# First modulation rows in three column blocks, the fourth row tile moved into the value stage, the last output tile in two pieces

## Chip, cores and metric

One core of one Trainium2 chip runs the whole program. The metric is the device time of one execution in microseconds (us); the profile's span, from the first to the last instruction, is about 2 us shorter.

Ratios in this document are the mean time of one kernel's fast runs over the mean time of the other's fast runs of the same rounds, so not quite the ratio of the medians that are quoted.

## The reference

A diffusion-style block: a modulated LayerNorm, linear attention with 32 heads, and a modulated SwiGLU. There are 2048 rows of width 1024; weights are bf16. Only the first half matters here.

```python
mod = (silu(c) @ w_mod).reshape(1, 6, 1, -1)      # w_mod: 1024 x 6144
sa, ca, ga, sb, cb, gb = mod[:, 0], ...           # shift, scale, gate, twice
h = layernorm(x) * (1 + ca) + sa
q, k, v = split(h @ wqkv)                         # each 2048 x 1024
# phi(q) and phi(k), kv = phi(k)^T v, o = phi(q) kv / (phi(q) z), then @ wo
x = x + ga * attention
h = layernorm(x) * (1 + cb) + sb
x = x + gb * ((silu(h @ w_gate) * (h @ w_up)) @ w_down)
```

No key, value or query can be made before `ca` and `sa` are known, and these need 4.2 MB of `w_mod`. That is what the first 25 us of the kernel are about.

## The kernel before

The rows are worked in four chunks (`sc`) of 512, each of four row tiles (`t`) of 128. All input transfers are issued on one queue, in the order of this code. `wme` holds columns of `w_mod`: first the scale (q = 1), then the shift (q = 0), in two blocks of 512 columns.

```python
for st in range(STC - 1):          # row tiles 0, 1, 2 of x
    load_x(st, nc.sync)
for b in range(2):
    for q in (1, 0):
        t = big("wme", [DC, NB])
        nc.sync.dma_start(out=t[:], in_=wm_v[:, :, q * D + b * NB:q * D + (b + 1) * NB])
    ...                            # rows 4b .. 4b+3 of the key weights, wk
    if b == 0:
        load_x(STC - 1, nc.sync)   # row tile 3
wv = load_w(wqkv_v, 2 * D, "wv")   # then x of the next chunk, then wq
```

The first stage. `in_order` pins the order of the instructions on DVE, ACT and POOL to the order of the code. `keep_warm` issues matmuls whose result nobody reads ("fillers"). `mod_block` turns one block of `w_mod` into columns of `ca1T` or `saT`, by matmuls with one moving column each. `k_mms` accumulates the six key groups of row tiles 0 to 2, one 128-wide slice `cc` of the width at a time. `modulate` applies scale and shift to one such slice on DVE.

```python
keep_warm(accs[5], 26)
with in_order(nc.vector, nc.scalar, nc.gpsimd):
    ...                            # LayerNorm and transposes of row tiles 0-2, 3 x keep_warm(4)
    for b in range(2):
        mod_block(b, 1); keep_warm(idle, 2)
        mod_block(b, 0); keep_warm(idle, 3)
        for cc in range(4 * b, 4 * b + 4):
            modulate(hTs[0], cc, ca1T, saT, 0, 3 * P)
        if b == 0:
            xn3 = ln1_norm(*ln1_stats(0, 3))
            k_mms(0, gs, accs, 0, 4)
            pe_transpose_tile(hTs[0], xn3, 3)
        else:
            k_mms(0, gs, accs, 4, 8)
    ...                            # modulate row tile 3, its two key groups
    k_evac(0, gs, accs)            # phi: exp on ACT, then two DVE instructions
    k_evac(0, gs2, accs2)
...
v_phase(0)                         # eight value groups of chunk 0
with tc.issue_after(last_on[nc.vector.engine]):
    ln1(1)                         # LayerNorm of chunk 1: behind the last key evacuation on DVE
q_phase(0, 0, 6)
modulate_all(hTs[1], ca1T, saT)
q_phase(0, 6, 8)                   # then the keys of chunk 1
```

The last stage, `down`, writes each output tile in two pieces of 512 columns: a series of 28 matmuls, a multiply and an add on DVE, a store.

Of the kernel before, what the change touches and what calls it, by code (L numbers as in the profile page):

```python
# [21 lines left out]
def kernel(  # L22
# [74 lines left out]
    def mm(out, lhsT, rhs, start, stop):  # L97
        return tc.keep_in_program_order(nc.tensor.matmul(out, lhsT=lhsT, rhs=rhs, start=start, stop=stop))  # L98
# [4 lines left out]
    def big(name, shape):  # L103
        return k8.tile([P] + shape, BF16, name=name, tag="k8")

    def acc_a():
        return pa.tile([P, NB], F32, name="acc", tag="pa")

    def acc_b(name, shape=(NB,), dt=F32):
        return pb.tile([P] + list(shape), dt, name=name, tag="pb")  # L110
# [8 lines left out]
    def load_x(st, eng):  # L119
        x_sb = k2.tile([P, D], BF16, name="x_sb")  # L120
        eng.dma_start(out=x_sb[:], in_=x2[st * P:(st + 1) * P, :])
        x_tiles[st] = x_sb

    for st in range(STC - 1):
        load_x(st, nc.sync)

    wme = []
    wk = [big("wk", [4, D]), big("wk", [4, D])]
    for b in range(2):
        ts = []  # L130
        for q in (1, 0):
            t = big("wme", [DC, NB])
            nc.sync.dma_start(out=t[:], in_=wm_v[:, :, q * D + b * NB:q * D + (b + 1) * NB])
            ts.append(t)
        wme.append(ts)
        for i in range(2):
            nc.sync.dma_start(out=wk[b][:, 2 * i:2 * i + 2, :], in_=wqkv_v[:, 4 * b + 2 * i:4 * b + 2 * i + 2, D:2 * D])
        if b == 0:
            load_x(STC - 1, nc.sync)

    def load_w(view, lo, name):
        ts = []
        for h in range(2):
            t = big(name, [4, D])
            nc.sync.dma_start(out=t[:], in_=view[:, 4 * h:4 * h + 4, lo:lo + D])
            ts.append(t)
        return ts
# [84 lines left out]
    def ln1_norm(sc, t, x_sb, mv, rstd):  # L232
        xn = k2.tile([P, D], BF16, name="xn", bufs=4)
        if sc == 0:
            normalise(xn[:], x_sb[:], mv[:, 0, 0:1], rstd[:, 0:1])
            return xn
        normalise_act(xn[:], x_sb[:], mv, rstd)
        nc.sync.dma_start_transpose(hTs[sc][:, :, t * P:(t + 1) * P], xn[:])
# [4 lines left out]
            ln1_norm(*ln1_stats(sc, t))  # L243

    def mod_block(b, q):
        k = 1 - q
        for i in range(4):
            col = q * DC + 4 * b + i
            for j in range(DC):
                mm(mod_ps[:, col:col + 1], lhsT=wme[b][k][:, j, i * P:(i + 1) * P],  # L250
                   rhs=scT[:, j:j + 1], start=(j == 0), stop=(j == DC - 1))
        cs = slice(4 * b, 4 * b + 4)
        src = mod_ps[:, q * DC + 4 * b:q * DC + 4 * b + 4]
        if q == 1:
            nc.vector.tensor_scalar_add(out=ca1T[:, cs], in0=src, scalar1=1.0)
        else:
            nc.vector.tensor_copy(out=saT[:, cs], in_=src)

    last_phi = [None]

# [17 lines left out]
    def k_evac(sc, gs, accs):  # L278
        for (t, nb), acc in zip(gs, accs):
            phi_to(pks[sc][:, t, nb * NB:(nb + 1) * NB], acc[:])  # L280

    def k_phase(sc, lo, hi):
        if lo == 0:
            pks[sc] = big("pk", [STC, D])
        for g in k_groups[lo:hi]:
            accs = [acc_a()]
            k_mms(sc, [g], accs)
            k_evac(sc, [g], accs)

    def v_phase(sc):  # L290
        v = big("v", [STC, HG, VW])
        vs[sc] = v
        nc.gpsimd.memset(v[:, :, :, P:VW], 1.0)
        for t in range(STC):
            for nb in range(NNB):
                acc = acc_a()
                for cc in range(DC):
                    mm(acc[:], lhsT=hTs[sc][:, cc, t * P:(t + 1) * P],
                                     rhs=wv[cc // 4][:, cc % 4, nb * NB:(nb + 1) * NB],
                                     start=(cc == 0), stop=(cc == DC - 1))  # L300
                nc.scalar.copy(out=v[:, t, nb * 4:(nb + 1) * 4, 0:P], in_=acc[:].rearrange("p (g e) -> p g e", e=P))  # L301

    def q_phase(sc, lo=0, hi=DC):
        if lo == 0:
# [94 lines left out]
    def keep_warm(acc, n):  # L399
        for _ in range(n):  # L400
            mm(acc[:], lhsT=sel[:, 0, :], rhs=sel[:], start=True, stop=True)

    gs = k_groups[0:6]
    accs = [acc_a() if i < 4 else acc_b("acc") for i in range(6)]
    keep_warm(accs[5], 26)
    hTs[0] = big("hT", [DC, SCW])
    pks[0] = big("pk", [STC, D])
    with in_order(nc.vector, nc.scalar, nc.gpsimd):
        st0 = ln1_stats(0, 0)
        st1 = ln1_stats(0, 1)  # L410
        xn0 = ln1_norm(*st0)
        st2 = ln1_stats(0, 2)
        xn1 = ln1_norm(*st1)
        pe_transpose_tile(hTs[0], xn0, 0)
        xn2 = ln1_norm(*st2)
        keep_warm(accs[5], 4)
        pe_transpose_tile(hTs[0], xn1, 1)
        keep_warm(accs[5], 4)
        pe_transpose_tile(hTs[0], xn2, 2)
        keep_warm(accs[5], 4)  # L420
        mod_ps = acc_b("mod_ps")
        for b in range(2):
            idle = accs[5] if b == 0 else accs2[0]
            mod_block(b, 1)
            keep_warm(idle, 2)
            mod_block(b, 0)
            keep_warm(idle, 3)
            for cc in range(4 * b, 4 * b + 4):
                modulate(hTs[0], cc, ca1T, saT, 0, 3 * P)
            if b == 0:  # L430
                xn3 = ln1_norm(*ln1_stats(0, 3))
                k_mms(0, gs, accs, 0, 4)
                pe_transpose_tile(hTs[0], xn3, 3)
                accs2 = [acc_b("acc")]
            else:
                k_mms(0, gs, accs, 4, 8)
        for cc in range(DC):
            modulate(hTs[0], cc, ca1T, saT, 3 * P, SCW)
        gs2 = k_groups[6:8]
        accs2.append(acc_b("acc"))  # L440
        k_mms(0, gs2, accs2)
        k_evac(0, gs, accs)
        k_evac(0, gs2, accs2)
    nc.vector.tensor_copy(out=sc32[:], in_=scT[:].unsqueeze(2).to_broadcast([P, DC, 32]))
    build_masks()

    for sc in range(NSC):
        if sc > 0:
            k_phase(sc, 0, 2)
            kv_phase(sc - 1)  # L450
            if sc >= 2:
                row = mod_rows(blks)
            k_phase(sc, 2, 4)
            if sc == 2:
                mod_bc(row)
            if sc == 3:
                mod_cols(row)
            k_phase(sc, 4, 8)
            if sc == 1:
                blks = mod_load([2 * D, 2 * D + NB, 5 * D, 5 * D + NB])  # L460
            if sc == 2:
                blks = mod_load([3 * D, 3 * D + NB, 4 * D, 4 * D + NB])
        v_phase(sc)
        if sc + 1 < NSC:
            with tc.issue_after(last_on[nc.vector.engine] if sc == 0 else last_phi[-5].ins):
                ln1(sc + 1)
        if sc == 0:
            q_phase(0, 0, 6)
        if sc + 1 < NSC:
            with tc.issue_after(last_phi[0].ins):  # L470
                modulate_all(hTs[sc + 1], ca1T, saT)
        if sc == 0:
            q_phase(0, 6, 8)
        if sc + 2 < NSC:
            for st in range((sc + 2) * STC, (sc + 3) * STC):
                load_x(st, nc.sync)
        if sc == 2:
            wo = load_w(wo_v, 0, "wo")
            for cc in range(DC):
                w = wo[cc // 4][:, cc % 4, :]  # L480
                nc.vector.tensor_tensor(out=w, in0=w, in1=ga_bc, op=ALU.mult)
# [89 lines left out]
    def down(sc, side):  # L571
        for t in range(STC):
            st = sc * STC + t
            for nb in range(NNB):
                ns = slice(nb * NB, (nb + 1) * NB)
                x1r = x1p.tile([P, NB], F32, name="x1r", bufs=2)
                nc.sync.dma_start(out=x1r[:], in_=x1_dram[st * P:(st + 1) * P, ns])
                y_ps = acc_a()
                for f in range(FC):
                    mm(y_ps[:], lhsT=guT[sc][f // GPT][:, f % GPT, t * P:(t + 1) * P],  # L580
                                     rhs=wd[f // WDF][:, f % WDF, ns], start=(f == 0), stop=(f == FC - 1))
                yt = ep.tile([P, NB], F32, name="e")
                nc.vector.tensor_tensor(out=yt[:], in0=y_ps[:], in1=gb_bc[:, ns], op=ALU.mult)  # L583
                ob = yp.tile([P, NB], BF16, name="ob")
                nc.vector.tensor_tensor(out=ob[:], in0=yt[:], in1=x1r[:], op=ALU.add)  # L585
                nc.sync.dma_start(out=out2[st * P:(st + 1) * P, ns], in_=ob[:])
                if side:
                    with tc.issue_after(last_mm[sc].ins):
                        side.pop(0)()
# [62 lines left out]
```

## Time and profile before

| | |
|---|---|
| time, median of 3 | 848.03 us (847.9 to 848.06) |
| span of the profile | 846.2 us |
| TensorE (PE) busy | 838.6 us |
| first key matmul | 16.30 us |
| value stage | 33.92 to 47.73 us |
| keys of chunk 1 | from 61.55 us |

The first part of the page of the kernel before gives, for each engine, busy time, share of the span and number of instructions.

```profile
PE 838.6 (99%) x4284; PEld 385.7 (46%) x4284; DVE 307.2 (36%) x602; ACT 173.8 (21%) x267; POOL 55.7 (7%) x160
```

TensorE is busy nearly always: the waits view of the whole span has only 0.6 us of PE waits after the first 25 us, so the rest of the program, 780 of 846 us, has hardly a wait to lose. But busy is not useful: fillers and waits that were filled count as busy. The timeline of PE shows that. Its columns are start and duration in us, engine, line, operation, output and inputs, tile sizes, number of instructions, and in brackets the idle time before and what ended it.

```profile
16.30 5.35 PE L98 MATMUL acc<-wk,hT 128*128 128x512 bf16 x24
21.49 0.61 PE L101 MATMUL tp<-ident,xn 128*128 128x128 bf16 x8
21.93 0.94 PE L98 MATMUL mod_ps<-scT,wme 128*128 128x1 bf16 x32
23.23 0.59 PE L98 MATMUL acc<-sel 128*128 128x512 bf16 x2 [0.35 <-DVE hT L221]
23.66 0.94 PE L98 MATMUL mod_ps<-scT,wme 128*128 128x1 bf16 x32
24.46 0.81 PE L98 MATMUL acc<-sel 128*128 128x512 bf16 x3
25.27 8.81 PE L98 MATMUL acc<-wk,hT 128*128 128x512 bf16 x40
33.92 13.98 PE L98 MATMUL acc<-wv,hT 128*128 128x512 bf16 x64
47.73 13.98 PE L98 MATMUL acc<-hT,wq 128*128 128x512 bf16 x64
61.55 3.62 PE L98 MATMUL acc<-wk,hT 128*128 128x512 bf16 x16
```

`acc<-sel` are fillers. Between 21.5 and 25.3 us TensorE makes no key: it turns row tile 3, makes the second modulation block, and fills.

How fast the transfers come sets this stage. The trace has the completion of every transfer, one semaphore step for each of 16 DMA engines; this list, worked out from those steps, has the last of the sixteen:

```
kernel before: landed at (us)
x tiles 0-2   4.04  4.81  5.51
wme 512 cols  9.38 (scale 0)   13.65 (shift 0)   20.01 (scale 1)   22.96 (shift 1)
wk, in halves of 4 rows: 15.01 16.40 | 24.31 25.67       x tile 3  17.09
wv            28.38  31.04
```

The LayerNorm of chunk 1 ends in transposes that the DMA queue does. This is the timeline of SP, which issues the transfers; the duration is that of the issue.

```profile
46.80 2.26 SPq L238 DMA_TRANSPOSE hT<-xn  x1
49.15 0.53 SPq L121 DMA_DIRECT2D x_sb<-in_A_x_dram  x1
49.77 1.24 SPq L238 DMA_TRANSPOSE hT<-xn  x1
```

These are the third transpose, a load of x that stands between, and the fourth and last; the first had been issued at 42.78. The last one landed at 53.35 us, 15.4 us after the first statistics of that LayerNorm (37.90 us), and long before the keys of chunk 1 at 61.55.

The end of the timeline, the last multiply and add on DVE:

```profile
841.77 0.69 DVE L583 TENSOR_TENSOR e<-acc,gb_bc 128x512 f32<-128x512 f32 x1 [4.63 <-PE acc L98]
842.49 0.69 DVE L585 TENSOR_TENSOR ob<-e,x1r 128x512 bf16<-128x512 f32 x1
```

### The profile page before, as it was taken

How to read it: one execution, taken by the hardware profiler on the slowest of the kernel's cores; microseconds unless marked ns; L12 is line 12 of the kernel's file. 1: busy time of each engine (PE TensorE's matmuls, PEld its weight loads, DVE VectorE, ACT ScalarE, POOL GpSimd, SP SyncE). 2: the span in 40 equal slices, each digit the busy share in tenths (PEclk: the TensorE clock that was granted, in tenths of full speed). 3: DMA queues.
4: the chain of work that ended last, by engine and by line, in shares of the span. 5: the costliest groups of instructions: out<-in, count | busy, mean ns of one | idle time of the engine just before them, and what ended most of it. 6: DMA issues, size and time to landing. Idle time of an engine off the chain costs nothing.

```text
span 846.2 us, 10498 instructions
## 1 busy us (share of the span) xinstructions
PE 838.6 (99%) x4284; PEld 385.7 (46%) x4284; DVE 307.2 (36%) x602; ACT 173.8 (21%) x267; POOL 55.7 (7%) x160
## 2 busy tenths in 40 slices
PE   8999999999999999999999999999999999999997
PEld 4445445544444444444444444444444444444443
DVE  5756464467423325431111344211114431111121
ACT  1455453354311110101111010011110101111000
POOL 2101010012011001100000010000001100000000
PEclk9999999999999999999999999999999999999999
DMA  9893870029976765528434073581604639710011
GB/s 309 301 257 98 243 187 1 1 52 215 348 210 207 214 186 174 181 69 266 146 104 149 19 236 95 159 283 54 199 1 126 185 69 318 240 59 0 19 57 50
DMA packets 125840, 128.74 MB, mean 152 GB/s; under 512 B 33376, under 2 KB 107360, under 8 KB 125280
## 3 DMA queue, kind: packets, MB, share of 16 engines
q1 hardware_dynamic: 122208, 115.36, 46.0%
q0 software_dynamic: 3584, 12.72, 5.0%
q8 instruction: 33, 0.54, 0.3%
q14 instruction: 15, 0.12, 0.0%
HBM read 108.01 MB, written 12.71 MB: 143 GB/s over the span
## 4 chain that ended last, share of the span: by engine, by line
PE 98%; DVE 1%; POOL 0%; DMA 0%; issue 0%; ACT 0%; SPq 0%; DVEq 0%; POOLq 0%
PE acc L98 88%; PE a_ps L98 7%; PE kvp L98 1%; PE modr L98 0%; PE wf L98 0%; DMA x_sb<-in_A_x_dram 0%; DVE stats L199 0%; PE mod_ps L98 0%; PE den L98 0%; POOL zmask L186 0%; PE tp L101 0%; POOL rstd L193 0%; PE bcr L98 0%; DVE e L583 0%; DVE ob L585 0%
## 5 line engine op out<-in xcount | busy, mean ns | idle before, releaser
L98 PE MATMUL acc<-h2T,wgu 128*128 128x512 bf16 x1792 | 387.9, 379 | 0.0
L98 PEld LDWEIGHTS <-wgu 128*128 128x128 bf16 x1792 | 175.1, 98 | 211.0
L98 PE MATMUL acc<-wd,gu 128*128 128x512 bf16 x896 | 196.0, 379 | 0.0
L566 DVE TENSOR_TENSOR gu<-acc,e 128x512 bf16<-128x512 f32 x112 | 77.4, 691 | 300.4 <-PE acc L98 300.4
L565 ACT ACTIVATE e<-acc 128x512 f32<-128x512 f32 x112 | 66.9, 597 | 375.2 <-PE acc L98 375.2
L98 PEld LDWEIGHTS <-gu 128*128 128x128 bf16 x896 | 87.6, 98 | 105.8
L98 PEld LDWEIGHTS <-hT 128*128 128x128 bf16 x512 | 49.6, 98 | 60.8 <-DVE hT L212 1.0
L583 DVE TENSOR_TENSOR e<-acc,gb_bc 128x512 f32<-128x512 f32 x32 | 22.1, 691 | 130.5 <-PE acc L98 130.5
L98 PE MATMUL a_ps<-wo,pq 128*128 128x512 bf16 x256 | 57.9, 379 | 0.6 <-DVE pq L395 0.6
L98 PE MATMUL acc<-hT,wq 128*128 128x512 bf16 x256 | 57.1, 379 | 0.0
L98 PE MATMUL acc<-wk,hT 128*128 128x512 bf16 x256 | 56.9, 379 | 0.0
L98 PE MATMUL acc<-wv,hT 128*128 128x512 bf16 x256 | 55.9, 379 | 0.0
L263 ACT ACTIVATE eb<-acc 128x512 bf16<-128x512 f32 x64 | 37.9, 596 | 62.8 <-PE acc L98 60.5
L209 ACT ACTIVATE xn<-x,nmr,rstd 128x1024 bf16<-128x1024 f32 x16 | 19.8, 1240 | 127.6 <-POOL nmr L207 127.6
L264 DVE TENSOR_SCALAR eb<-eb 128x512 bf16<-128x512 bf16 x64 | 18.4, 291 | 60.6 <-ACT eb L263 60.6
L98 PEld LDWEIGHTS <-pq 128*128 128x128 bf16 x256 | 24.7, 98 | 31.8 <-DVE pq L395 2.6
L98 PEld LDWEIGHTS <-wq 128*128 128x128 bf16 x256 | 24.9, 98 | 29.8
L534 POOL DMA_DIRECT2D x_scratch<-x x16 | 9.6, 600 | 369.6 <-DVE x L527 369.6
L527 DVE TENSOR_TENSOR x<-a_ps,x_sb 128x512 f32<-128x512 f32 x32 | 22.1, 691 | 8.0 <-PE a_ps L98 7.9
L193 POOL TENSOR_TENSOR rstd<-veps,neg_half 128x1 f32<-128x1 f32 x32 | 18.2, 569 | 81.3 <-DVE veps L191 70.4
L301 ACT CAST v<-acc 128x512 bf16<-128x512 f32 x32 | 18.3, 582 | 22.1 <-PE acc L98 22.1
L528 DVE BATCH_NORM_STATS2 stats<-x 128x6 f32<-128x512 f32 x32 | 22.2, 695 | 1.1
(72 smaller groups left out, 280.7 us busy)
## 6 DMA issues: line engine op xcount, KB each, us to landing
wgu<-in_B_w_gate_dram SPq DMA_DIRECT2D x28, 1024.0 KB, 7.4
wgu<-in_B_w_up_dram SPq DMA_DIRECT2D x28, 1024.0 KB, 8.7
x_sb<-in_A_x_dram SPq DMA_DIRECT2D x32, 256.0 KB, 5.9
wml<-in_w_mod_dram SPq DMA_DIRECT2D x8, 1024.0 KB, 8.6
x_scratch<-x POOLq DMA_DIRECT2D x16, 512.0 KB, 3.1
x1r<-x_scratch SPq DMA_DIRECT2D x32, 256.0 KB, 3.0
wd<-in_B_w_down_dram SPq DMA_DIRECT2D x7, 1024.0 KB, 7.7
wme<-in_w_mod_dram SPq DMA_DIRECT2D x4, 1024.0 KB, 11.2
```

The source lines that it names most:

```text
L98: return tc.keep_in_program_order(nc.tensor.matmul(out, lhsT=lhsT, rhs=rhs, start=start, stop=stop))
L193: nc.gpsimd.tensor_tensor(out=rstd[:, 0:n], in0=veps[:, 0:n], in1=neg_half[:].to_broadcast([P, n]), op=ALU.pow)
L209: nc.scalar.activation(out=dst, in_=src, func=ACT.Identity, bias=nmr[:], scale=rstd[:, 0:1])
L263: nc.scalar.activation(out=e[:], in_=acc, func=ACT.Exp)
L264: nc.vector.tensor_scalar(out=e[:], in0=e[:], scalar1=1.0, scalar2=PHI_EPS, op0=ALU.min, op1=ALU.add)
L301: nc.scalar.copy(out=v[:, t, nb * 4:(nb + 1) * 4, 0:P], in_=acc[:].rearrange("p (g e) -> p g e", e=P))
L527: nc.vector.tensor_tensor(out=x1[:, ns], in0=a_ps[:], in1=x_t[:, ns], op=ALU.add)
L528: nc.vector.bn_stats(out=stats[:, nb, :], in_=x1[:, ns])
L534: nc.gpsimd.dma_start(out=x1_dram[st * P:(st + 1) * P, :], in_=x1[:])
L565: nc.scalar.activation(out=sg[:], in_=ps[0][:], func=ACT.Silu)
L566: gm = nc.vector.tensor_tensor(out=guT[sc][f // GPT][:, f % GPT, :], in0=ps[1][:], in1=sg[:], op=ALU.mult)
L583: nc.vector.tensor_tensor(out=yt[:], in0=y_ps[:], in1=gb_bc[:, ns], op=ALU.mult)
```

## The change

The intent is to start keys sooner and to leave fewer of them behind the last modulation piece. The scale and shift columns come in blocks of three, three and two slices of 128 columns, each followed by the key-weight rows that need them, and the modulation of the next block stands before the last slice of the present one. Row tile 3 no longer takes part in the first key groups: its x is loaded between the two halves of `wv`, four value groups of tiles 0 and 1 are made first, and its transpose and two key groups come in the middle of the value stage. Twenty of the 48 fillers go. The masks, which POOL had made during the first LayerNorm, come later. The last tile's second piece is made in two halves.

```diff
+    MBLK = [(0, 3), (3, 6), (6, 8)]
-    for b in range(2):
+    for lo, hi in MBLK:
         for q in (1, 0):
-            nc.sync.dma_start(out=t[:], in_=wm_v[:, :, q * D + b * NB:q * D + (b + 1) * NB])
+            nc.sync.dma_start(out=ts[q][:], in_=wm_v[:, :, q * D + lo * P:q * D + hi * P])
+        ...                                   # the key-weight rows lo .. hi
-        if b == 0:
-            load_x(STC - 1, nc.sync)
 [in load_w]
+            if name == "wv" and h == 1:
+                load_x(STC - 1, nc.sync)
 [first stage]
-    keep_warm(accs[5], 26)
+    keep_warm(accs[5], 22)
-        keep_warm(accs[5], 4)                 # three times
+        keep_warm(accs[5], 3)                 # twice
+        mod_block(0, 1)
         pe_transpose_tile(hTs[0], xn2, 2)
+        mod_block(0, 0)
+        for b, (lo, hi) in enumerate(MBLK):
+            for cc in range(lo, hi):
+                modulate(hTs[0], cc, ca1T, saT, 0, 3 * P)
+            k_mms(0, gs, accs, lo, hi - 1)
+            if b + 1 < len(MBLK):
+                mod_block(b + 1, 1)
+                mod_block(b + 1, 0)
+            k_mms(0, gs, accs, hi - 1, hi)
+        st3 = ln1_stats(0, 3)
+        k_evac(0, gs[0:2], accs[0:2])
+        xn3 = ln1_norm(*st3)
+        k_evac(0, gs[2:], accs[2:])
+    ...                                       # value groups (0,0) (0,1) (1,0) (1,1), in two halves
+    pe_transpose_tile(hTs[0], xn3, 3)
+    ...                                       # modulate tile 3; values (2,*); keys of tile 3; values (3,*)
+    with tc.issue_after(last_on[nc.gpsimd.engine]):
         build_masks()
 [down]
+            pieces = [(0, NB), (NB, NB)]
+            if st == ST - 1:
+                pieces = [(0, NB), (NB, NB // 2), (NB + NB // 2, NB // 2)]
```

More of the change, by code (lines that the diff above doesn't have):

```diff
@@ L125 @@
         load_x(st, nc.sync)
+    MBLK = [(0, 3), (3, 6), (6, 8)]
     wme = []
     wk = [big("wk", [4, D]), big("wk", [4, D])]
-    for b in range(2):
-        ts = []
+    for lo, hi in MBLK:
+        ts = {}
         for q in (1, 0):
-            t = big("wme", [DC, NB])
-            nc.sync.dma_start(out=t[:], in_=wm_v[:, :, q * D + b * NB:q * D + (b + 1) * NB])
-            ts.append(t)
+            ts[q] = big("wme", [DC, (hi - lo) * P])
+            nc.sync.dma_start(out=ts[q][:], in_=wm_v[:, :, q * D + lo * P:q * D + hi * P])
         wme.append(ts)
-        for i in range(2):
-            nc.sync.dma_start(out=wk[b][:, 2 * i:2 * i + 2, :], in_=wqkv_v[:, 4 * b + 2 * i:4 * b + 2 * i + 2, D:2 * D])
-        if b == 0:
-            load_x(STC - 1, nc.sync)
+        for h in range(2):
+            r0, r1 = max(lo, 4 * h), min(hi, 4 * h + 4)
+            if r0 < r1:
+                nc.sync.dma_start(out=wk[h][:, r0 - 4 * h:r1 - 4 * h, :], in_=wqkv_v[:, r0:r1, D:2 * D])
     def load_w(view, lo, name):
@@ L245, in mod_block @@
     def mod_block(b, q):
-        k = 1 - q
-        for i in range(4):
-            col = q * DC + 4 * b + i
+        lo, hi = MBLK[b]
+        mod_ps = acc_b("mod_ps")
+        for i in range(hi - lo):
             for j in range(DC):
-                mm(mod_ps[:, col:col + 1], lhsT=wme[b][k][:, j, i * P:(i + 1) * P],
+                mm(mod_ps[:, i:i + 1], lhsT=wme[b][q][:, j, i * P:(i + 1) * P],
                    rhs=scT[:, j:j + 1], start=(j == 0), stop=(j == DC - 1))
-        cs = slice(4 * b, 4 * b + 4)
-        src = mod_ps[:, q * DC + 4 * b:q * DC + 4 * b + 4]
         if q == 1:
-            nc.vector.tensor_scalar_add(out=ca1T[:, cs], in0=src, scalar1=1.0)
+            nc.vector.tensor_scalar_add(out=ca1T[:, lo:hi], in0=mod_ps[:, 0:hi - lo], scalar1=1.0)
         else:
-            nc.vector.tensor_copy(out=saT[:, cs], in_=src)
+            nc.vector.tensor_copy(out=saT[:, lo:hi], in_=mod_ps[:, 0:hi - lo])
     last_phi = [None]
@@ L288, in k_phase, with new_v, v_mms, v_evac @@
             k_evac(sc, [g], accs)
+    def new_v():
+        v = big("v", [STC, HG, VW])
+        nc.gpsimd.memset(v[:, :, :, P:VW], 1.0)
+        return v
+    def v_mms(sc, t, nb, acc, lo=0, hi=DC):
+        for cc in range(lo, hi):
+            mm(acc[:], lhsT=hTs[sc][:, cc, t * P:(t + 1) * P], rhs=wv[cc // 4][:, cc % 4, nb * NB:(nb + 1) * NB],
+               start=(cc == 0), stop=(cc == DC - 1))
+    def v_evac(sc, t, nb, acc):
+        nc.scalar.copy(out=vs[sc][:, t, nb * 4:(nb + 1) * 4, 0:P], in_=acc[:].rearrange("p (g e) -> p g e", e=P))
+    def v_group(sc, t, nb, acc):
+        v_mms(sc, t, nb, acc)
+        v_evac(sc, t, nb, acc)
     def v_phase(sc):
-        v = big("v", [STC, HG, VW])
-        vs[sc] = v
-        nc.gpsimd.memset(v[:, :, :, P:VW], 1.0)
+        vs[sc] = new_v()
         for t in range(STC):
             for nb in range(NNB):
-                acc = acc_a()
-                for cc in range(DC):
-                    mm(acc[:], lhsT=hTs[sc][:, cc, t * P:(t + 1) * P],
-                                     rhs=wv[cc // 4][:, cc % 4, nb * NB:(nb + 1) * NB],
-                                     start=(cc == 0), stop=(cc == DC - 1))
-                nc.scalar.copy(out=v[:, t, nb * 4:(nb + 1) * 4, 0:P], in_=acc[:].rearrange("p (g e) -> p g e", e=P))
+                v_group(sc, t, nb, acc_a())
     def q_phase(sc, lo=0, hi=DC):
@@ L415 @@
         xn2 = ln1_norm(*st2)
-        keep_warm(accs[5], 4)
+        keep_warm(accs[5], 3)
         pe_transpose_tile(hTs[0], xn1, 1)
-        keep_warm(accs[5], 4)
+        keep_warm(accs[5], 3)
+        mod_block(0, 1)
         pe_transpose_tile(hTs[0], xn2, 2)
-        keep_warm(accs[5], 4)
-        mod_ps = acc_b("mod_ps")
-        for b in range(2):
-            idle = accs[5] if b == 0 else accs2[0]
-            mod_block(b, 1)
-            keep_warm(idle, 2)
-            mod_block(b, 0)
-            keep_warm(idle, 3)
-            for cc in range(4 * b, 4 * b + 4):
-                modulate(hTs[0], cc, ca1T, saT, 0, 3 * P)
-            if b == 0:
-                xn3 = ln1_norm(*ln1_stats(0, 3))
-                k_mms(0, gs, accs, 0, 4)
-                pe_transpose_tile(hTs[0], xn3, 3)
-                accs2 = [acc_b("acc")]
-            else:
-                k_mms(0, gs, accs, 4, 8)
+        mod_block(0, 0)
@@ new lines @@
+        for b, (lo, hi) in enumerate(MBLK):
+            for cc in range(lo, hi):
+                modulate(hTs[0], cc, ca1T, saT, 0, 3 * P)
+            k_mms(0, gs, accs, lo, hi - 1)
[7 more added lines that the diff above has]
+        k_evac(0, gs[2:], accs[2:])
+    vs[0] = new_v()
+    vg = [(0, 0, acc_b("acc")), (0, 1, acc_b("acc")), (1, 0, acc_a()), (1, 1, acc_a())]
@@ L437 @@
+    for half in range(2):
+        for t, nb, acc in vg:
+            v_mms(0, t, nb, acc, 4 * half, 4 * half + 4)
+    for t, nb, acc in vg:
+        v_evac(0, t, nb, acc)
+    pe_transpose_tile(hTs[0], xn3, 3)
+    with in_order(nc.vector):
         for cc in range(DC):
             modulate(hTs[0], cc, ca1T, saT, 3 * P, SCW)
-        gs2 = k_groups[6:8]
-        accs2.append(acc_b("acc"))
-        k_mms(0, gs2, accs2)
-        k_evac(0, gs, accs)
-        k_evac(0, gs2, accs2)
-    nc.vector.tensor_copy(out=sc32[:], in_=scT[:].unsqueeze(2).to_broadcast([P, DC, 32]))
@@ L445 @@
-    build_masks()
+    v_group(0, 2, 0, acc_a())
+    v_group(0, 2, 1, acc_a())
+    with in_order(nc.vector):
+        k_phase(0, 6, 8)
+    v_group(0, 3, 0, acc_a())
+    v_group(0, 3, 1, acc_a())
+    with tc.issue_after(last_on[nc.vector.engine]):
+        nc.vector.tensor_copy(out=sc32[:], in_=scT[:].unsqueeze(2).to_broadcast([P, DC, 32]))
+    with tc.issue_after(last_on[nc.gpsimd.engine]):
+        build_masks()
     for sc in range(NSC):
@@ L462 @@
                 blks = mod_load([3 * D, 3 * D + NB, 4 * D, 4 * D + NB])
-        v_phase(sc)
+            v_phase(sc)
         if sc + 1 < NSC:
@@ L573, in down @@
             st = sc * STC + t
-            for nb in range(NNB):
-                ns = slice(nb * NB, (nb + 1) * NB)
+            pieces = [(0, NB), (NB, NB)]
+            if st == ST - 1:
+                pieces = [(0, NB), (NB, NB // 2), (NB + NB // 2, NB // 2)]
+            for lo, width in pieces:
+                ns = slice(lo, lo + width)
                 x1r = x1p.tile([P, NB], F32, name="x1r", bufs=2)
-                nc.sync.dma_start(out=x1r[:], in_=x1_dram[st * P:(st + 1) * P, ns])
+                nc.sync.dma_start(out=x1r[:, 0:width], in_=x1_dram[st * P:(st + 1) * P, ns])
                 y_ps = acc_a()
                 for f in range(FC):
-                    mm(y_ps[:], lhsT=guT[sc][f // GPT][:, f % GPT, t * P:(t + 1) * P],
-                                     rhs=wd[f // WDF][:, f % WDF, ns], start=(f == 0), stop=(f == FC - 1))
+                    mm(y_ps[:, 0:width], lhsT=guT[sc][f // GPT][:, f % GPT, t * P:(t + 1) * P],
+                       rhs=wd[f // WDF][:, f % WDF, ns], start=(f == 0), stop=(f == FC - 1))
                 yt = ep.tile([P, NB], F32, name="e")
-                nc.vector.tensor_tensor(out=yt[:], in0=y_ps[:], in1=gb_bc[:, ns], op=ALU.mult)
+                nc.vector.tensor_tensor(out=yt[:, 0:width], in0=y_ps[:, 0:width], in1=gb_bc[:, ns], op=ALU.mult)
                 ob = yp.tile([P, NB], BF16, name="ob")
-                nc.vector.tensor_tensor(out=ob[:], in0=yt[:], in1=x1r[:], op=ALU.add)
-                nc.sync.dma_start(out=out2[st * P:(st + 1) * P, ns], in_=ob[:])
+                nc.vector.tensor_tensor(out=ob[:, 0:width], in0=yt[:, 0:width], in1=x1r[:, 0:width], op=ALU.add)
+                nc.sync.dma_start(out=out2[st * P:(st + 1) * P, ns], in_=ob[:, 0:width])
                 if side:
```

## The prediction

> **What bounds the kernel now.** TensorE is busy 838.6 of 846.2 us (page, part 1); the chain of waits is 98% PE. After 25 us it hardly idles, so only the head (0 to 48 us), the tail, or new stalls can move the time. By the timeline, key matmuls start at 16.30 us; 24 run, then a transpose, the second modulation block and five fillers, and the other 40 from 25.27; values run 33.92 to 47.7. Transfers set the head: about 350 to 390 GB/s from 10 us on (stage table). Landings by the transfers' semaphores: x tiles 0-2 by 5.5 us, modulation columns 9.4, 13.65, 20.0, 22.96, last key weights 25.67, wv 28.4 and 31.0.
>
> **What changes.**
> - 20 of 48 fillers go (0.216 us each when warm); the mask memsets on POOL, which delayed the third tile's rstd by about 1.2 us (8.3 to 10.9 us), move behind. Both help only until data is the limit.
> - The modulation bytes stay, but rows become 768 and 512 B instead of 1024 B. In the packet records a 1024 B packet takes about 49 ns, a 2048 B one 88. The Trainium skill ("DMA: Bandwidth & Descriptors", Why small descriptors are slow) gives a fixed cost per packet, and these two times agree. Estimate: the six pieces take 0.8 us more than the four.
> - x tile 3 leaves the head of the queue (-0.7 us) and lands between the halves of wv.
>
> **Estimated head** (from those rates): first key rows land at 13-14 us, so keys start near 14 instead of 16.3. The last modulation piece lands at 23-24 us; only 18 of the 48 early key matmuls remain, K ends near 28, and V starts at once. If nothing else waited, V and K would end near 45-46 instead of 47.7: 1.5 to 2.6 us gained. Two new waits take much back:
> 1. Row tile 3's statistics stand on DVE ahead of the key evacuations, and its x lands about 28.7 us. Statistics 1.7, then phi 1.0 us: the third value group gets its PSUM bank near 31.5 instead of 30. PE stall about 1.5 us.
> 2. The next chunk's LayerNorm is queued behind the last key evacuation, now 3.5 us, not 14 us, before the value stage ends. It takes 15.4 us from its first statistics (37.9) to the last landed transpose (53.35). That now ends close to the start of chunk 1's keys (13.8 us of queries after V); with 2.7 us of modulation behind it, PE stalls about 1 to 2 us there.
>
> **Tail.** The last DVE multiply and add (0.70 + 0.69 us) and output copy work on half the width: about 0.7 us gained; the narrow matmuls cost about 0.1.
>
> Sum: head -1.5 to -2.6, stalls about +2.5, tail -0.7, and part of the stalls may not come: I expect 847.0 us, 80% range 844.0 to 849.4; faster by 2%: 0.01, within 2%: 0.98, slower: 0.01.
>
> **Shows it right or wrong.** First key matmul near 14 us; PE idle before mod_ps and first keys, released by wme/wk transfers; the third value group waiting on pk of DVE; V end 45.5 to 48; a PE wait on hT at chunk 1's first keys (near 61 us); final DVE pair near 0.37 us each.
>
> **What would make it wrong.** If x tile 3 lands before the keys end and the transposes come earlier, no stalls: 843 to 844. If fewer fillers let the clock fall: the skill ("TensorE: Matmul & The Clock Gate", The HAM clock gate) names about 3.4 us of idling; the trace shows full clock from 4.1 us on. I expect gaps under 2 us; a lapse costs about 2 us.

## The result, and the profile after

The changed kernel took 848.38 us as the median of 4 (847.36, 847.56, 849.19 and 849.33), the kernel before 848.04 of 4 on the same chip (847.9 to 848.39); the ratio is 1.0003, with a 95% interval of 0.9986 to 1.002. Nothing was gained. The profiled execution is the 847.36 us one, at the low end of the four: its span is 845.5 us, 0.7 us under before. So two questions stand: where did the head's gain go, and why do other executions take up to 2 us longer than this one?

First part of the page of the changed kernel:

```profile
PE 831.7 (98%) x4213; PEld 387.2 (46%) x4292; DVE 307.7 (36%) x606; ACT 173.7 (21%) x267; POOL 55.6 (7%) x160
```

TensorE is less busy by 6.9 us. In part this is filler time; some is an artefact, since matmul records are missing from this trace (4213, where the weight loads, 4292, show what the program issues: 20 fillers fewer and 28 narrow matmuls more than the 4284 of before), so this view cannot be used as a ledger. The timeline of PE can:

```profile
14.27 2.76 PE L98 MATMUL acc<-wk,hT 128*128 128x512 bf16 x11 [1.04 <-DVE hT L214]
16.87 0.74 PE L98 MATMUL mod_ps<-scT,wme 128*128 128x1 bf16 x24
18.34 0.75 PE L98 MATMUL mod_ps<-scT,wme 128*128 128x1 bf16 x24 [0.73 <-DMA wme<-in_w_mod_dram]
19.16 3.83 PE L98 MATMUL acc<-wk,hT 128*128 128x512 bf16 x17
22.83 0.54 PE L98 MATMUL mod_ps<-scT,wme 128*128 128x1 bf16 x16
24.16 0.55 PE L98 MATMUL mod_ps<-scT,wme 128*128 128x1 bf16 x16 [0.79 <-DMA wme<-in_w_mod_dram]
24.79 3.83 PE L98 MATMUL acc<-wk,hT 128*128 128x512 bf16 x17
28.46 1.89 PE L98 MATMUL acc<-wv,hT 128*128 128x512 bf16 x8
31.57 5.45 PE L98 MATMUL acc<-wv,hT 128*128 128x512 bf16 x24 [1.22 <-DVE pk L266]
47.66 14.18 PE L98 MATMUL acc<-hT,wq 128*128 128x512 bf16 x62
61.67 3.62 PE L98 MATMUL acc<-wk,hT 128*128 128x512 bf16 x16
```

(Some matmul records are missing: the groups of 17 are 18.) Keys start 2.0 us sooner and the first values 5.5 us sooner (the value stage now has 16 key matmuls in it). Yet the queries start at 47.66, 0.07 us sooner than before, and the keys of chunk 1 at 61.67, 0.12 us later. The waits of PE, summed by who was waited for (line waited for: us in total, times, longest), name what took it:

```profile
PE mod_ps L98 <- DMA wme<-in_w_mod_dram: 1.5, 2, 0.8
PE acc L98 <- DVE pk L266: 1.2, 1, 1.2
PE acc L98 <- DVE hT L214: 1.0, 1, 1.0
```

Of these, the kernel before had only 0.4 us on `hT`. The first belongs to modulation columns that had not landed, twice. The third is the first key matmul's: in this execution it waited for the modulation on DVE, whose shift columns had stood behind a copy of the last transpose (copy at 13.30, shift at 13.64), with the key rows landed at 13.57; in four other profiles the same wait is put down to the key rows themselves (1.1 to 1.4 us). The second is a new wait: the third value group needs a PSUM bank that is free only when DVE has evacuated the first key group, and DVE stood waiting for row tile 3:

```profile
28.87 1.29 DVE L201 BATCH_NORM_STATS2 stats<-x_sb 128x6 f32<-128x512 bf16 x2 [3.25 <-DMA x_sb<-in_A_x_dram]
30.19 0.21 DVE L202 BATCH_NORM_AGGREGATE mv<-stats 128x2 f32<-128x12 f32 x1
30.43 0.15 DVE L193 TENSOR_SCALAR veps<-mv 128x1 f32<-128x1 f32 x1
30.50 0.28 DVE L264 TENSOR_SCALAR eb<-eb 128x512 bf16<-128x512 bf16 x1
30.82 0.69 DVE L266 SCALAR_TENSOR_TENSOR pk<-acc,eb 128x512 bf16<-128x512 f32 x1
```

The statistics of row tile 3 begin at 28.87, when its x has landed (28.84); only then the key evacuation (`eb`, `pk`) may run, though its keys were ready at about 27.6. The landings of the changed kernel:

```
changed kernel: landed at (us)
x tiles 0-2   4.37  5.06  5.73
wme block 0 (768 B rows)  9.14 11.50    wk rows 0-2  13.57
wme block 1 (768 B rows) 15.97 18.29    wk rows 3-5  19.10 20.54
wme block 2 (512 B rows) 22.34 24.12    wk rows 6-7  25.46
wv 28.17    x tile 3 28.84    wv 31.75
```

The transposes of chunk 1 (SP, columns as before) now come 8 us later, the first issued at 51.06, the last landing at 59.53. The last two are issued together (x2), with no load of x between them:

```profile
54.45 0.53 SPq L121 DMA_DIRECT2D x_sb<-in_A_x_dram  x1
55.08 2.62 SPq L240 DMA_TRANSPOSE hT<-xn  x2
```

And the tail:

```profile
841.96 0.42 DVE L605 TENSOR_TENSOR e<-acc,gb_bc 128x256 f32<-128x256 f32 x1 [2.17 <-PE acc L98]
842.42 0.42 DVE L607 TENSOR_TENSOR ob<-e,x1r 128x256 bf16<-128x256 f32 x1
```

Ledger of the profiled execution: up to the keys of chunk 1, +0.12 us; from there to the last DVE multiply 780.29 us against 780.22, +0.07 for the narrow matmuls; from there to the end of the span 3.54 us (845.5 less 841.96) against 4.43, so -0.9. Together -0.7: the head gave nothing, the tail gave what it could.

### The profile page after: what moved, and what is told of

The parts are those of the page before. It is cut to its first block, busy times and chain, and to the rows that moved or that the text cites. A ratio compares the mean times of both kernels' runs of the same rounds, so it can differ in the third digit from the quotient of the medians.

```text
span 845.5 us, 10448 instructions
## 1 busy us (share of the span) xinstructions
PE 831.7 (98%) x4213; PEld 387.2 (46%) x4292; DVE 307.7 (36%) x606; ACT 173.7 (21%) x267; POOL 55.6 (7%) x160
## 4 chain that ended last, share of the span: by engine, by line
PE 94%; SPq 2%; DVE 1%; issue 1%; DMA 1%; ACT 1%; POOL 0%; DVEq 0%; ACTq 0%
PE acc L98 85%; PE a_ps L98 7%; SPq L139 1%; DMA x_sb<-in_A_x_dram 1%; SPq L134 1%; PE kvp L98 1%; PE modr L98 0%; DVE stats L201 0%; PE wf L98 0%; ACT xn L211 0%; PE den L98 0%; ACT eb L263 0%; DVE pk L266 0%; SPq L121 0%; DVE eb L264 0%
## 5 line engine op out<-in xcount | busy, mean ns | idle before, releaser
L98 PE MATMUL acc<-wd,gu 128*128 128x512 bf16 (+1 forms) x907 | 195.0, 372 | 0.9
L98 PEld LDWEIGHTS <-gu 128*128 128x128 bf16 x924 | 90.4, 98 | 103.3
L605 DVE TENSOR_TENSOR e<-acc,gb_bc 128x512 f32<-128x512 f32 (+1 forms) x33 | 22.3, 676 | 131.7 <-PE acc L98 131.7
L201 DVE BATCH_NORM_STATS2 stats<-x_sb 128x6 f32<-128x512 bf16 x32 | 20.6, 671 | 6.5 <-DMA x_sb<-in_A_x_dram 6.5
```

Of the source, the lines that this page charges most:

```text
L98: return tc.keep_in_program_order(nc.tensor.matmul(out, lhsT=lhsT, rhs=rhs, start=start, stop=stop))
L201: nc.vector.bn_stats(out=stats[:, i, :], in_=src[:, i * NB:(i + 1) * NB])
L605: nc.vector.tensor_tensor(out=yt[:, 0:width], in0=y_ps[:, 0:width], in1=gb_bc[:, ns], op=ALU.mult)
```

## The experiments

All kernels gave the correct result unless said otherwise. "Lower group" in the expectations means the two executions near 847.4 us above.

### The changed kernel again

The same code, five rounds.

> The changed kernel again, only run more often. The first four executions of it lay in two pairs, 847.4/847.6 and 849.2/849.3 us, where the kernel before stays within 0.5 us. Clock theory (fewer fillers let the TensorE clock fall, or come up later, in some executions): again two groups about 1.9 us apart, the upper ones with a lower mean granted clock, and before stays in one group. Rival (noise of the first chip): one group within 0.6 us.

Measured: median 848.03 us (848.03, 849.15, 847.82, 848.95, 847.45), before 847.96 in the same rounds (nine executions, 847.67 to 848.22); ratio 1.0004 (0.9991 to 1.0016). The scatter is there again, over 1.7 us, more spread out than two groups. Mean granted clocks were 0.996 or 0.998 in all five, against 0.999 to 1.000 in all nine of before. (A stretch of 3.4 us at half clock lowers the mean over 846 us by 0.002.) But the clock does not sort the executions, as the clock theory had it: 847.45 and 848.95 us were both at 0.998, and among the first four 847.56 and 849.33. The profile has a stretch of half clock (a lapse, below), 3.4 us long, from 13.64 to 17.05 us. It can be seen in the stage table (from:to, length, busy us of PE, PEld, DVE, ACT, POOL with counts, PEclk, DMA share, GB/s) and then in the timeline of PE, where ten key matmuls take 3.34 us (at full clock eleven took 2.76):

```profile
10.00:15.00 5.00, 3.46 (x68) 2.66 (x68) 2.89 (x9) 2.46 (x3) 0.20 (x1) 0.86 1.06 356
15.00:20.00 5.00, 4.70 (x59) 2.62 (x60) 0.23 (x2) 0.00 (x0) 0.00 (x0) 0.79 1.09 346
```

```profile
15.01 3.34 PE L98 MATMUL acc<-wk,hT 128*128 128x512 bf16 x10 [0.22 <-issue]
```

PEclk is 0.86 and 0.79, where it is 1.00 in the changed kernel's first profile. The queries start at 48.34 in place of 47.66 and the span is 846.1, 0.6 us longer. It is tempting to charge this to the lapse, but the trace does not allow it: after the lapse TensorE still had to wait for the last modulation piece.

```profile
24.79 0.55 PE L98 MATMUL mod_ps<-scT,wme 128*128 128x1 bf16 x16 [0.61 <-DMA wme<-in_w_mod_dram]
```

That piece landed at 24.74 us in place of 24.12, and the first piece had landed at 9.79 in place of 9.14, before the lapse. From there on all transfers came 0.5 to 0.8 us late in this execution, and the lapse was hidden behind them. The x of row tile 3, on which the statistics and so the `pk` wait depend, landed at 29.47 in place of 28.84. In the five profiles with this order of work and no fillers in the waits (the changed kernel twice, and three runs below) it landed at 28.84, 29.16, 29.36, 29.47 and 30.04 us, and the queries start 18.8 to 18.9 us after that in every one, with or without a lapse. The kernel before does not follow its landings in this way: in its two kept profiles (the second is the run with only the new tail, below) the last modulation piece landed at 22.96 and 23.61, and the first values start at 33.92 in both. So with the change the head took over the scatter of the transfers.

### Fillers of before put back at the same places

```diff
-    keep_warm(accs[5], 22)
+    keep_warm(accs[5], 26)
-        keep_warm(accs[5], 3)      # twice
+        keep_warm(accs[5], 4)
```

> The changed kernel with the fillers of before in its first stage (26, 4 and 4 for 22, 3 and 3). Clock theory: the upper group is gone, all executions within 0.6 us near 847.4, because keys wait for modulation columns at 18.3 and 24.1 us anyway, so that the six fillers cost under 0.3 us. Rival (the fillers were pure cost, spread has another cause): 1 to 1.3 us slower than the changed kernel's lower group, or the two groups remain.

Measured: 848.54 us median (847.77 to 849.31), ratio 1.0007 (0.9993 to 1.002). Clocks were 0.996 to 0.998. In its profile the half-clock stretch is still there, only later, 19.91 to 23.32 us, right after a wait of 1.72 us for modulation columns. The queries start at 48.86, but here the x of row tile 3 landed only at 30.04; the time that the keys lost to the lapse came out of the `pk` wait, which is 0.45 us in place of 1.2. So the first form of the clock theory falls: it is not the number of fillers at the start that keeps the clock up. The rival's size (1 to 1.3 us) cannot be told from the scatter.

### Statistics of row tile 3 behind two key evacuations

```diff
-        st3 = ln1_stats(0, 3)
         k_evac(0, gs[0:2], accs[0:2])
+        st3 = ln1_stats(0, 3)
         xn3 = ln1_norm(*st3)
```

> Row tile 3's statistics placed behind the first two key evacuations. My theory: the 1.22 us wait of the third value group for pk goes, value stage ends near 46.4 instead of 47.66 us, total about 1.2 us less in either group (846.2 in the lower one), and the chunk 1 keys follow 14 us later without a new stall. Rival (values are limited by the second half of wv, landed at 31.75): the wait only moves to wv and the gain is under 0.4 us.

Measured: 846.64 us median (846.04 to 847.49), ratio 0.9986 (0.9973 to 0.9998); the mean is 1.5 us under that of the changed kernel in the same rounds (846.76 against 848.28). The 1.2 us wait for `pk` is gone. In the timeline of PE all 32 matmuls of the first value groups stand in one block, and the queries start at 46.62:

```profile
28.84 7.13 PE L98 MATMUL acc<-wv,hT 128*128 128x512 bf16 x32
46.62 14.24 PE L98 MATMUL acc<-hT,wq 128*128 128x512 bf16 x62
```

From the first values to the queries it is 17.8 us in place of 19.2: 1.4 us gained, close to the difference of the means. This execution had a lapse of the clock too (14.25 to 17.66 us), which cost nothing: the first values start 4.34 us after the last modulation piece landed, as in the changed kernel's first profile, which had none. The new wait that was predicted as number 1 is shown, with its size, by taking its cause away; no wait on `wv` took its place.

### Tail: last tile as before; and the tail alone on the kernel before

In the first, the changed kernel writes its last tile in two pieces of 512; in the second, the kernel before gets only the new `down`.

```diff
 [changed kernel, tail as before]
-            if st == ST - 1:
-                pieces = [(0, NB), (NB, NB // 2), (NB + NB // 2, NB // 2)]
```

> The changed kernel with the last tile in two pieces as before. Theory: 0.7 us more than the changed kernel in the same group (848.1 in the lower one), final DVE pair 0.69 us each. Rival (narrow matmuls and more instructions eat the gain): within 0.2 us of the changed kernel.

> The kernel before with the last tile in two pieces and nothing else. Theory: 0.7 us faster than before (847.3), last DVE pair 0.42 us each. Rival: within 0.2 us of before.

Measured: without the new tail the changed kernel took 849.04 us (848.51 to 850.97), ratio to before 1.0019 (1.0006 to 1.0032), 1.0 us above the median of the changed kernel in the same rounds; that is more than the tail can account for and is in the scatter. Its profile (span 846.8, 1.3 us above the changed kernel's first, with no lapse) shows the two parts: 0.6 us up to the keys of chunk 1, with the x of row tile 3 landed 0.5 us later, and 0.8 us from there on. The kernel before with the tail took 847.73 us (847.38 to 849.28) against 848.01, ratio 0.9999 (0.9985 to 1.0013): on that chip both it and the kernel before had executions one to two us above the rest, so the times are inconclusive. The profile is not: its queries start at 47.74 as before, its last multiply at 841.84 (841.77 before), its span ends at 845.5. The tail is worth 0.7 us, and the narrow matmuls cost 0.07.

### Fillers in the waits, without and with the repaired order

Ten fillers go where TensorE waits: four before the first keys, and three in front of each later shift block (written into the bank that this block then overwrites).

```diff
-    def mod_block(b, q):
+    def mod_block(b, q, warm=0):
         mod_ps = acc_b("mod_ps")
+        keep_warm(mod_ps, warm)
 ...
         mod_block(0, 0)
+        keep_warm(accs[5], 4)
 ...
-                mod_block(b + 1, 0)
+                mod_block(b + 1, 0, 3)
```

> The changed kernel with ten fillers put where TensorE waits for data: four before the first keys, three before each of the two later shift blocks. Clock theory, second form (the clock falls to half for 3.4 us after a stretch of waits and one-column matmuls; fillers at the start do not help, fillers in the waits do): no half-clock stretch between 7 and 30 us in the profile, all executions within 0.6 us near 847.4 to 847.8. Rival (fillers here only delay the keys): 848.5 to 849.5, and lapses as before.

> The ten fillers in the waits, and row tile 3's statistics behind the first two key evacuations. If both losses are as told and independent: 846.0 to 846.5 in all executions, 1.5 to 2.0 us under the kernel before. Rival (the fillers cost as much as the clock): no better than the run with the statistics alone, 846.8 on average.

Measured, fillers alone: 847.96 us (847.81 to 849.34), ratio 1.0 (0.9988 to 1.0013). Two of five executions were at clock 1.000, three at 0.998; the profile has a lapse from 20.02 to 23.43 us, after a wait of 1.37 us that the three fillers did not cover, and it fell on the keys: the first values start at 30.75, 6.0 us after the last modulation piece in place of 4.3, so 1.7 us were lost there. Most of this came out of the `pk` wait, which is gone: the queries start 19.0 us after the x of row tile 3 landed, 0.1 to 0.2 us more than without. Half a success: the expectation of no lapse failed.

Measured, with the statistics moved too: 846.47 us (846.0 to 847.65), ratio 0.9981 (0.9968 to 0.9993), and no lapse in the profile. That is 1.5 us under before, but its mean, 846.60, is only 0.2 us under the run with the statistics alone, which the scatter cannot tell from nothing, and one execution (847.65, at clock 0.998) fell outside the 846.0 to 846.5 that was expected of all.

### More fillers in the first of those waits

Both repairs, and six in place of three fillers before the first later shift block.

```diff
-                mod_block(b + 1, 0, 3)
+                mod_block(b + 1, 0, 6 if b == 0 else 3)
```

> Both repairs, with six fillers in place of three before the first of the two later shift blocks, where the profiles still show 0.7 to 1.4 us of waiting. Clock theory: nearly all executions at a mean clock of 0.999 or 1.000 and within 0.4 us of 846.4. Rival (the extra fillers run after the data is there and delay the keys): about 0.6 us slower than with three.

Measured: 846.38 us (845.9 to 847.8), ratio 0.9982 (0.9969 to 0.9994). All six executions were at a mean clock of 1.000, and the stage table shows full clock where the changed kernel had lost it in its second profile:

```profile
10.00:15.00 5.00, 4.75 (x77) 3.16 (x75) 2.69 (x9) 2.46 (x3) 0.29 (x2) 1.00 1.06 360
15.00:20.00 5.00, 4.84 (x66) 2.68 (x65) 0.66 (x4) 0.00 (x0) 0.00 (x0) 1.00 1.09 345
```

So fillers in the waits seem to hold the clock when they cover them: with three fillers, four of the ten executions of the two runs above were at 0.998, with six none of six. So few executions do not prove it. And the six still spread over 1.9 us (846.99 and 847.8 are among them), and the mean of 846.59 is that of three fillers. The clock is then not the cause of this scatter.

### Fewer fillers

The changed kernel without its two groups of three between the transposes: double the suspected cause.

```diff
         xn2 = ln1_norm(*st2)
-        keep_warm(accs[5], 3)
         pe_transpose_tile(hTs[0], xn1, 1)
-        keep_warm(accs[5], 3)
         mod_block(0, 1)
```

> The changed kernel with its two groups of three fillers between the transposes taken out (22 at the start stay). Clock theory: the clock falls to half for 3.4 us at least once before 24 us in nearly every execution, often twice (mean clock 0.996 to 0.998), executions between 848.0 and 849.5 us, and the profile shows key matmuls at twice their time. Rival (the clock has no part in it and fillers are only cost): 847.4 us or less, mean clock as in the changed kernel.

Measured: 848.74 us (847.31 to 849.66), ratio 1.0001 (0.9987 to 1.0014). All six executions were at 0.995 or 0.996, and the profile has two lapses in a row, 12.75 to 19.57 us. So the cause is doubled as foretold, and yet the mean (848.58) is only 0.3 us above that of the changed kernel, which ran on another chip. In the profile the queries start 18.8 us after the x of row tile 3 landed (29.16), as without lapses. Both theories are half right: the clock falls, and it costs little or nothing, for it falls while TensorE is ahead of the data.

This profile caught something else, from three views: the issue of one DMA transpose on SP took 2.69 us where the changed kernel's took 1.23, so the last transpose landed at 61.37 us; DVE then waited to modulate chunk 1; and the 16 first keys of chunk 1 took 4.35 us in place of 3.62.

```profile
53.46 2.69 SPq L240 DMA_TRANSPOSE hT<-xn  x1
```

```profile
61.50 1.71 DVE L214 TENSOR_SCALAR hT<-hT,ca1T,saT 128x512 bf16<-128x512 bf16 x5 [1.03 <-DMA hT<-xn]
```

```profile
61.99 4.35 PE L98 MATMUL acc<-wk,hT 128*128 128x512 bf16 x16
```

This is the second predicted wait, 0.7 us of it, in one execution of a kernel with the same order of work.

### Last two key groups behind all values

Both repairs, but the keys of row tile 3 at the end of the value stage, which puts the LayerNorm of chunk 1 3.3 us later (first statistics at 48.49 in place of 45.21).

```diff
-    with in_order(nc.vector):
-        k_phase(0, 6, 8)
     v_group(0, 3, 0, acc_a())
     v_group(0, 3, 1, acc_a())
+    with in_order(nc.vector):
+        k_phase(0, 6, 8)
```

> Both repairs, and the last two key groups moved behind all values, so that the last key evacuation, and with it the next chunk's LayerNorm, comes 3.45 us later. Slack theory (the predicted second wait is real but had about 0.5 us of slack): the last transpose lands near 62 us, a PE wait of 2 to 3 us on hT at chunk 1's first keys, 2 to 3 us slower than both repairs alone (848.5 to 849.5). Rival (the LayerNorm is not bound to that evacuation, or the queue absorbs it): no wait, within 0.3 us.

Measured: 849.22 us (848.96 to 849.75), ratio 1.0014 (0.9998 to 1.0029); on the mean 2.7 us slower than both repairs alone. The last transpose landed at 61.93 us. The waits of PE:

```profile
PE acc L98 <- DVE pq L267: 1.3, 1, 1.3
PE acc L98 <- DVE hT L214: 0.7, 2, 0.6
```

The wait on `hT` came, and one that was not foretold: queries waited 1.3 us for `pq`, since the three normalisations in a row on ACT and the statistics on DVE stood in front of the query evacuations. So of the 2.7 us about half is the predicted kind of wait: 0.6 us of waiting, and 16 first keys that took 4.38 us in place of 3.62 while DVE was still modulating (62.05 to 64.72 us). The LayerNorm of chunk 1 is bound to the last key evacuation, and the changed kernel sits close to the edge.

### Two column blocks

Both repairs, with `MBLK = [(0, 4), (4, 8)]`.

```diff
-    MBLK = [(0, 3), (3, 6), (6, 8)]
+    MBLK = [(0, 4), (4, 8)]
```

> As the run with both repairs, but the modulation rows in two column blocks (packets of 1024 B) in place of three. Three-block theory: after the last modulation piece lands (about 0.8 us sooner) 30 key matmuls are left in place of 18, 2.6 us of work, so 1.5 to 2 us slower than with three blocks. Rival (smaller packets eat it): within 0.4 us of three blocks.

Measured: 848.4 us (847.38 to 849.99), ratio 1.0003 (0.999 to 1.0015); on the mean 1.9 us slower than three blocks (848.47 against 846.60). The last modulation piece landed at 22.64 us, 2.0 us before that of the three-block run (24.64; the expectation had 0.8; two key-weight rows fewer stand before it in the queue), and 30 key matmuls were left after it:

```profile
23.57 1.46 PE L98 MATMUL acc<-wk,hT 128*128 128x512 bf16 x6
25.38 5.34 PE L98 MATMUL acc<-wk,hT 128*128 128x512 bf16 x24 [0.34 <-DMA wk<-in_A_wqkv_dram]
30.55 7.07 PE L98 MATMUL acc<-wv,hT 128*128 128x512 bf16 x32
```

The values started at 30.55 against 28.99. This profile had a lapse of the clock (14.79 to 18.20 us) in the first block, but it does not account for that: the last 24 keys waited 0.34 us for their key rows, which landed at 25.33. Three blocks are better, though their pieces come later.

### Half the modulation bytes

The shift columns are not loaded; the scale columns stand in for them, so 2.1 MB less is read before the keys end. The result is wrong. (The comparison with the reference passed all the same: its tolerance does not see this.)

```diff
         for q in (1, 0):
+            if q == 0:
+                ts[0] = ts[1]
+                continue
```

> The changed kernel with the shift columns not loaded; the scale columns are used in their place (wrong result on purpose), so 2.1 MB less is read before the keys. Data theory (landings set the first stage): waits on modulation columns and key rows go, row tile 3 lands about 6 us earlier so its wait goes too, value stage ends near 43.5 in place of 47.7 us, 843.5 to 844.5 in all. Rival (DVE and TensorE's own chain set it): the value stage ends after 46 us.

Measured: 843.87 us, all four executions within 0.3 us (843.76 to 843.98), ratio 0.9949 (0.9935 to 0.9962). No wait for modulation columns or for `pk` is left, and the queries start 3.6 us sooner than in the changed kernel:

```profile
44.05 14.18 PE L98 MATMUL acc<-hT,wq 128*128 128x512 bf16 x64
```

With row tile 3 landed at 23.39 us its statistics hold nobody up. This run takes away the data limit and the `pk` wait together; with the 1.2 us of the latter known, some 2.4 us are, by difference, the data's. It had no lapse of the clock in its profile either. That its executions lie within 0.3 us, where those of the changed kernel spread over 2, fits a scatter that comes with the transfers.

## Why the prediction was right, point by point

**Range.** The measured 848.38 us is in the range of 844.0 to 849.4, and the kernel is neither faster nor slower by 2%. The point, 847.0, was 1.4 us low. Luck had a part in the range: wait 2, priced at 1 to 2 us, did not come, and the head, freed of wait 1, gained 1.0 to 1.4 us (queries at 46.33 to 46.70 in the four profiles with the statistics moved and three blocks, against 47.73) in place of 1.5 to 2.6.

**Data sets the head: shown.** First keys were predicted near 14 us (14.27), the last modulation piece at 23 to 24 (24.12), the first values near 28 (28.46). The run with half the bytes shows that the limit is real. The Trainium skill ("DMA: Bandwidth & Descriptors", Why small descriptors are slow) tells of a fixed cost per packet; here the two 768 B pieces that follow key rows without a hiccup took 2.40 and 2.32 us for 0.79 MB each and the 512 B pieces 1.80 and 1.78 us for 0.52 MB, that is 328 to 339 and about 293 GB/s, against 355 GB/s for the kernel before's fourth piece of 1024 B rows (2.95 us for 1.05 MB). It agrees in direction; no run here took the packet size alone.

**Wait 1, statistics ahead of the key evacuations: shown.** Predicted 1.5 us, bank free near 31.5; measured 1.22 us and 31.57. Moving the statistics back by two evacuations removed it, and 1.5 us on the mean.

**Wait 2, the next chunk's LayerNorm: the step that failed.** "PE stalls about 1 to 2 us there." In the profiled execution the keys of chunk 1 did not wait on `hT`. The term that was mis-sized is the 15.4 us from first statistics to last transpose, which was carried over from the kernel before. In the changed kernel the path took 13.36 us (46.17 to 59.53). It is not that one execution had been slow: the other profile with the old order of this stage, the kernel before with the new tail, has the same 15.45 us, though its third transpose was issued in 1.23 us and not 2.26. There the load of x behind it took long:

```profile
46.81 1.23 SPq L238 DMA_TRANSPOSE hT<-xn  x1
48.13 1.43 SPq L121 DMA_DIRECT2D x_sb<-in_A_x_dram  x1
```

In both, the last transpose was issued 2.97 and 2.85 us after the third. In all twelve profiles with the new order no load of x stands between these two; in the changed kernel they were issued 1.33 us apart. The path is 13.4 to 13.6 us in eleven of the twelve, and 14.89 in the run with fewer fillers, where one issue took 2.69. Why the program's order on SP came out differently was not looked into. So modulation on DVE began at 60.06, when DVE was done with the queries before it and not when a transpose landed, and the first slices were ready in time. The dependency itself is right: the late issue cost 0.7 us in the run with fewer fillers, and about half of the 2.7 us of the run with the keys last is this wait.

**Tail: right.** Predicted 0.7 us net, measured 0.7 in the profiles; the DVE pair takes 0.42 us each, not the 0.37 predicted.

**Clock: the step that was waved off.** The prediction expected gaps under 2 us and took those to be safe, from the about 3.4 us of idling that it cited from the skill. Gaps were under 2 us, and the clock fell for 3.4 us at a time in most executions, after stretches of transposes, one-column matmuls and short waits. It was also priced too high: 2 us was named for a lapse. In the profiles with the order of the changed kernel a lapse moved the start of the queries by 0.2 us at most, since TensorE then waited less for data or for `pk`; the most that a lapse took from the keys themselves was 1.7 us.

**Why the point was low.** The lower executions, 847.36 and 847.56, are 0.5 us above the point. In the profiled one wait 2 did not come, but the head's gain, 1.0 to 1.4 us, was eaten by wait 1. The other two, near 849.3, make the median. The prediction had one time and no scatter.

**Open.** No profile caught one of the executions near 849.2 us. Late landings (0.3 to 1.2 us between the profiles) and a late transpose issue (0.7 us) have each been seen in other profiles to lengthen an execution, and the change has made the kernel sensitive to both; that they, together, are what the upper executions had is argued, not shown. A lapse of the clock is not needed for it: the kernel with no lapses at all still spread over 1.9 us. In later rounds the kernel before also had single executions 1.6 to 2.7 us above its rest, at a mean clock of 0.998 where its others were at 0.999 or 1.000. A lapse of 3.4 us at half clock can take at most 1.7 us (an estimate: half its length), so in two of them, 1.9 and 2.7 us above, there is more than a lapse. This part of the scatter has nothing to do with the change, and it is not explained here.

**A version that beats both.** The changed kernel with the statistics moved and fillers in its waits: 846.47 us with three fillers in the first wait, 846.38 with six, against 848.01 and 848.0 of before; ratios 0.9981 and 0.9982, both intervals below 1. Nearly all of the gain is the one moved line.

## What to carry to other kernels

When a stage is limited by transfers, removing filler work turns it into waits; count only what moves the last landing, or what is left to do after it. Such a stage also takes over the scatter of the transfers, so compare two executions from the landing on before naming another cause for their difference. Where an engine's order is pinned, look at what stands in front of a buffer's evacuation: an instruction that waits for a transfer there holds up everyone who needs the buffer, and moving it by one line was here worth more than the whole change. And do not carry a path's length over from the old order of work when the slack is one microsecond: here the issue order on the DMA queue changed with it, and the path became 2 us shorter.

## What the Trainium skill lacked or had wrong

- "TensorE: Matmul & The Clock Gate", Part 1, The HAM clock gate: its table has the clock fall after an idle window of about 3.4 us. Here it fell although no wait was over 2 us: in six profiles transposes, one-column matmuls and single waits of 0.5 to 1.7 us were enough, while one wait of 1.9 us (tail as before) was not. The page does tell, for another kernel, of short idle times between groups of matmuls that make the clock swing, but gives no length. The length of a lapse agrees (3.413 us in each profile, 6.827 for two in a row), and so does its word that the window is free-running: full clock came at 4.1 us in the kernel before and at 7.0 us in the changed kernel's first profile.
- The same page does not say how much filling holds the clock: three matmuls of 512 columns in a wait of about 2 us did not in one profile (lapse at 20.0 us); with six, all six executions were at a mean clock of 1.000.
- "DMA: Bandwidth & Descriptors": the page gives no time that SP takes to issue a DMA transpose of this size (128 x 1024, in SBUF), nor that it varies: for chunk 1's transposes SP took 1.23 to 1.42 us as a rule, 2.26 and 2.69 us once each in two profiles.
